# VectorE's exponentials in an attention kernel: seven passes in place of eight, on 16-bit halves

## The chip, the cores and the metric

The kernel runs on one core of a Trainium2 chip. The metric is the device time of one execution in microseconds, less is better. Of the kernel before, three runs gave 2255.68, 2258.31 and 2261.54 us; the median is 2258.31 us.

The engines of the core are named as the profile names them: PE is TensorE (matmuls; PEld its weight loads), ACT is ScalarE, DVE is VectorE, POOL is GpSimd, SP is the engine that issues most DMAs.

## The reference

Four transformer-like blocks follow one another, each a layer norm, an attention and a residual sum. The first and third use a sliding window of 256 positions, the second and fourth full attention without a mask. There are 2048 positions, 640 features, 32 heads of 20 features.

```python
def _A_ref(x, wqkv, wo):
    B, S, D = x.shape
    H = 32; Dh = D // H; W = 256
    ...
    scores = jnp.einsum("bhqd,bhkd->bhqk", q, k) * (Dh ** -0.5)
    idx = jnp.arange(S)
    mask = (idx[:, None] - idx[None, :] >= 0) & (idx[:, None] - idx[None, :] < W)
    scores = jnp.where(mask[None, None], scores, -1e9)
    p = _softmax(scores, axis=-1)
    o = jnp.einsum("bhqk,bhkd->bhqd", p, v)
    return (lambda x, *d: x.transpose(*d))(o, 0, 2, 1, 3).reshape(B, S, D) @ wo
...
x = x + _A_ref(_layernorm(x, axis=-1), A_wqkv, A_wo)
x = x + _B_ref(_layernorm(x, axis=-1), B_wqkv, B_wo)
x = x + _A_ref(_layernorm(x, axis=-1), A_wqkv, A_wo)
x = x + _B_ref(_layernorm(x, axis=-1), B_wqkv, B_wo)
```

`_B_ref` is the same without the mask. All inputs are bf16. What counts here is that every score of the two full blocks goes through an exponential: 2 x 32 x 2048 x 2048 of them.

## The kernel before, in words

**Units.** The work of the attention is cut into units (`Unit`, L672): one block of the network `l`, one chunk `c` of 512 queries, one group `g` of four heads; some units of the second and fourth block are cut further by keys (`PARTS`, L40). For one head and 128 keys a score matmul (L1316) writes a score block, 128 keys by 512 queries in f32, which fills one of the eight PSUM banks. ScalarE takes three score blocks with one instruction, computes the exponential and writes bf16 (L1347). Where bank 6 is free and no other task is ready, it takes four in one instruction, which writes into the tile `ka`. The value matmuls (L1380) multiply the exponentials with the values and sum in bank 7; a column of ones in the values gives the sum of the exponentials. At the end of a unit bank 7 is copied out (L864) and a "tail" divides by that sum (L1053 to L1092).

**Ticks.** The main loop (L1279) makes one tick of each such ScalarE instruction: it issues the score matmuls, the exponential, and then, as far as a credit reaches, pieces of the other work: projections of queries, keys and values (L294 to L298, evacuated by VectorE at L321), output projections (L566), layer norms, tails. Bank 5 (early) and bank 6 serve this other work. All orders are fixed when the program is built: every engine runs its own list in order, and waits for the others by semaphores.

**The blocks that go aside.** ScalarE's exponentials are many, so a fixed set of score blocks of the full attention goes to VectorE: `self.aside` (L676 to L686) lists two blocks a unit in the second network block and four or six in the fourth. Together these are 48 and 106 blocks, handled in 24 and 53 pairs. `t_side` (L897) is the generator that issues VectorE's passes for one pair. A `yield` with a number says what a pass costs in credit (0.7 or 1.2); `side_step` (L956) goes on with the generator only while the credit is positive. The credit grows by 0.4 a tick in the second network block, and by 1.1 (0.95 in the last chunk) in the fourth (L1402). In the second block of the network the score blocks come with a tile of the main loop at fixed ticks (L1320 to L1330); in the fourth they have a score matmul of their own into bank 6 (L912), issued on odd ticks when the bank is free (L1286), and the bank then counts as taken for two ticks. At the end of the unit `side_done` (L998) issues whatever passes of the unit are still missing, and the value matmuls of L1389 take the results.

**The eight passes of a pair, before.** VectorE has no exponential, so e^s is built as 2^t with t = s times log2(e). Two passes (L918, one for each score block of 512 columns) scale the scores by 2^23 log2(e) and write them as 32-bit integers, so that the upper 9 bits are the whole part and the lower 23 the fraction. L923 masks the fraction out and puts an exponent to it, so that it can be read as an f32; L928 masks the whole part out and shifts it to where an exponent is. Four passes with two inputs follow on 1024 columns of f32: L933, L937 and L941 evaluate a polynomial in the fraction, and L949 does the last step of it, multiplies by the power of two and writes bf16. The three work tiles `xi`, `xm`, `xw` are 1024 columns of f32 each; they lie in `raw_o` in the second network block and in `xnT` tiles in the fourth, and the results in `raw_o`, `ka` or `qa`, which is how the profile names them.

Of the kernel before, what the change touches and what calls it, by code (L numbers as in the profile page):

```python
# [9 lines left out]
BF16 = mybir.dt.bfloat16  # L10
F32 = mybir.dt.float32
I32 = mybir.dt.int32
ALU = mybir.AluOpType
ACT = mybir.ActivationFunctionType

# [8 lines left out]
C = 512  # L24
NC = S // C
EPS = 1e-5
SCALE = DH ** -0.5
# [2 lines left out]

E23 = 2.0 ** 23
LOG2E = 1.4426950408889634
EA, EB, EC, ED = -0.10468731, 1.17604568, 0.83196789, 0.24582313
KA = 18
SIDE_RATE = 1.1
QA = 4
# [8 lines left out]
def kernel(  # L47
# [58 lines left out]
    op = ps[:, 7, :]  # L106
# [23 lines left out]
    def load_wop(w, dense):  # L130
# [8 lines left out]
    nc.gpsimd.affine_select(  # L139
        out=ident[:], in_=ident[:], compare_op=ALU.not_equal, fill=1.0,  # L140
        base=0, pattern=[[-1, P]], channel_multiplier=1,
# [5 lines left out]
    for m, b, ge in (  # L147
# [5 lines left out]
        nc.gpsimd.affine_select(  # L153
            out=v, in_=v, compare_op=ALU.is_ge if ge else ALU.is_gt, fill=0.0,
            base=0, pattern=[[1 if ge else -1, P]], channel_multiplier=-1 if ge else 1,
# [4 lines left out]
    def other_constants():  # L160
# [7 lines left out]
        for u in range(2):  # L168
# [4 lines left out]
            nc.vector.tensor_tensor(  # L173
                out=sp16[r], in0=sp32[r, 0, :], in1=sp32[r, 1, :], op=ALU.add
            )
# [215 lines left out]
    def t_ln(l, c):  # L391
# [3 lines left out]
        for n in (1, 0):  # L395
# [6 lines left out]
        nc.gpsimd.tensor_scalar(  # L402
            out=rstd[:], in0=mv[:, :, 1], scalar1=EPS, scalar2=1.0, op0=ALU.add, op1=ALU.mult
        )
        nc.gpsimd.tensor_tensor(out=rstd[:], in0=rstd[:], in1=nhalf[:], op=ALU.pow)
        yield ("wait", 2)
        nmr = lnp.tile([P, 4], F32, name="nmr", tag="nmr")
        nc.vector.scalar_tensor_tensor(
            out=nmr[:], in0=mv[:, :, 0], scalar=-1.0, in1=rstd[:], op0=ALU.mult, op1=ALU.mult
        )  # L410
# [476 lines left out]
    def side_early():  # L887

        b = part_o["t"]
        side["tiles"] = [b[:, 2 * n : 2 * n + 2, :].rearrange("p a b -> p (a b)") for n in range(3)]  # L890
        side["out"] = deque(
            b[:, n, :].bitcast(BF16).rearrange("p (a b) -> p a b", a=2) for n in (6, 7)
        )
        side["gen"] = t_side()
        side_step(False)

    def t_side():  # L897

        V = nc.vector
        while aside:  # L900
            u = aside[0]
            for pair in range(len(u.aside) // 2):
                while id(u) not in loaded or (u.l == 3 and not side["late"]):
                    yield None
                for i in range(2):
                    yield "bank"
                    xi, xm, xw = side["tiles"]
                    if u.l == 3:
                        mseq[0] += 1
                        mfree[6] = (state["tick"] + 2, mseq[0])  # L910
                        kc, j = u.aside[2 * pair + i]
                        nc.tensor.matmul(  # L912
                            ps[:, 6, :], lhsT=u.k(kc, j), rhs=u.q(j, 0, 4), start=True, stop=True
                        )
                        side["psum"] = ps[:, 6, :]
                    scored = side.setdefault("scored", {})
                    scored[id(u)] = scored.get(id(u), 0) + 1
                    V.tensor_scalar(  # L918
                        out=xi.bitcast(I32)[:, i * C : (i + 1) * C], in0=side["psum"],
                        scalar1=SCALE * LOG2E * E23, scalar2=-128.0 * E23, op0=ALU.mult, op1=ALU.max,  # L920
                    )
                    yield 0.7
                V.tensor_scalar(  # L923
                    out=xm.bitcast(I32), in0=xi.bitcast(I32), scalar1=0x7FFFFF, scalar2=0x3E800000,
                    op0=ALU.bitwise_and, op1=ALU.bitwise_or,
                )
                yield 0.7
                V.tensor_scalar(  # L928
                    out=xi.bitcast(I32), in0=xi.bitcast(I32), scalar1=0x7F800000,
                    scalar2=0x40000000, op0=ALU.bitwise_and, op1=ALU.bitwise_xor,  # L930
                )
                yield 0.7
                V.scalar_tensor_tensor(  # L933
                    out=xw, in0=xm, scalar=EA, in1=xm, op0=ALU.add, op1=ALU.mult
                )
                yield 1.2
                V.scalar_tensor_tensor(  # L937
                    out=xm, in0=xw, scalar=EB, in1=xm, op0=ALU.mult, op1=ALU.add
                )
                yield 1.2  # L940
                V.scalar_tensor_tensor(  # L941
                    out=xw, in0=xw, scalar=EC, in1=xm, op0=ALU.add, op1=ALU.mult
                )
                yield 1.2
                while not side["out"]:
                    yield None
                pt = side["out"].popleft()
                po = pt.rearrange("p a b -> p (a b)")
                V.scalar_tensor_tensor(  # L949
                    out=po, in0=xw, scalar=ED, in1=xi, op0=ALU.add, op1=ALU.mult  # L950
                )
                side_out.setdefault(id(u), []).append(pt)
                yield 1.2
            aside.popleft()

    def side_step(bank):  # L956
# [246 lines left out]
    with tc.manual_schedule():  # L1203
# [75 lines left out]
        while ended is None or t < ended + 8:  # L1279
# [3 lines left out]
            if t < len(tiles) or banks:  # L1283
# [58 lines left out]
                while i < n_b:  # L1342
                    b0 = cur[i][3]
                    k = i
                    while k < n_b and cur[k][3] == b0:
                        k += 1
                    nc.scalar.activation(  # L1347
                        out=pt[:, i:k, b0 * P :], in_=sp[:, i:k, b0 * P :],
# [56 lines left out]
            if t > 0 and masked is not None:  # L1405
                cur_, pt_ = masked
                i = 0
                while i < len(cur_):
# [5 lines left out]
                    for b in ((3,), (1, 2), (0,))[m] if split else ():  # L1414
                        if b < b0:
# [4 lines left out]
                            out=v, in_=v, compare_op=ALU.is_gt if later else ALU.is_ge, fill=0.0,  # L1420
# [3 lines left out]
                    if split and m != 1:  # L1424
# [5 lines left out]
                            out=pt_[:, i:k, cols], in0=pt_[:, i:k, cols], in1=mv_, op=ALU.mult  # L1430
                        )
                    elif m is not None and not split:
# [5 lines left out]
                            out=pt_[:, i:k, cols], in0=pt_[:, i:k, cols], in1=mv_, op=ALU.mult  # L1438
# [38 lines left out]
```

## Time and profile before

One execution was profiled. Its span, from the first to the last instruction, is 2253.6 us; the trace records no longer time for it. The table gives the three stretches that matter: the first is that of the second network block's aside passes, the last that of the fourth's.

| | whole span | 493 to 1310 us | 1310 to 1600 us | 1600 to 2240 us |
|---|---|---|---|---|
| length, us | 2253.6 | 817 | 290 | 640 |
| ACT busy, us | 2159.6 | 795.9 | 281.2 | 635.4 |
| PE busy, us | 1946.9 | 704.5 | 246.5 | 543.9 |
| DVE busy, us | 1253.3 | 427.1 | 100.2 | 448.1 |
| POOL busy, us | 484.2 | 170.7 | 71.3 | 0.0 |
| granted PE clock | 0.99 | 1.00 | 1.00 | 0.99 |

The rows of the aside passes, as the profile groups them (both tiles together):

| line | what | count | mean, us |
|---|---|---|---|
| L918 | scale, f32 in PSUM to int32, 512 columns | 154 | 0.69 |
| L923, L928 | mask, int32, 1024 columns | 77 each | 0.69 |
| L933, L937, L941 | two inputs, f32, 1024 columns | 77 each | 1.22 |
| L949 | two inputs, f32 to bf16, 1024 columns | 77 | 1.22 |

How to read it: "busy" is the time in which an engine runs at least one instruction. PE's instructions overlap and their ends are modelled, so 86% busy is not 86% of its peak. A wait is put down to the semaphore that came last. An engine that is idle costs nothing unless the path that ends last goes through it.

### The profile page before, as it was taken

How to read it: one execution, taken by the hardware profiler on the slowest of the kernel's cores; microseconds unless marked ns; L12 is line 12 of the kernel's file. 1: busy time of each engine (PE TensorE's matmuls, PEld its weight loads, DVE VectorE, ACT ScalarE, POOL GpSimd, SP SyncE). 2: the span in 40 equal slices, each digit the busy share in tenths (PEclk: the TensorE clock that was granted, in tenths of full speed). 3: DMA queues.
4: the chain of work that ended last, by engine and by line, in shares of the span. 5: the costliest groups of instructions: out<-in, count | busy, mean ns of one | idle time of the engine just before them, and what ended most of it. 6: DMA issues, size and time to landing. Idle time of an engine off the chain costs nothing.

```text
span 2253.6 us, 71223 instructions
## 1 busy us (share of the span) xinstructions
PE 1946.9 (86%) x30991; PEld 775.9 (34%) x30991; DVE 1253.3 (56%) x2150; ACT 2159.6 (96%) x1736; POOL 484.2 (21%) x950
## 2 busy tenths in 40 slices
PE   8999998988888888888888888898888888888887
PEld 4444443334333333333333443342322222222222
DVE  6656564436454555455553643242577667776666
ACT  7899899999999999999899999999999999999997
POOL 6674544201111124111331123312000000000000
PEclk9999999999999999999999999999999999999999
DMA  6233323422111233012320143113211111111100
GB/s 196 74 102 84 91 78 91 104 70 69 54 34 28 65 91 87 15 34 62 97 78 15 23 115 95 29 26 89 64 52 31 31 40 34 31 31 47 39 19 16
DMA packets 88408, 137.15 MB, mean 61 GB/s; under 512 B 20766, under 2 KB 63486, under 8 KB 88094
## 3 DMA queue, kind: packets, MB, share of 16 engines
q1 hardware_dynamic: 68878, 79.43, 13.2%
q0 software_dynamic: 19216, 53.17, 8.1%
q8 instruction: 242, 3.96, 0.8%
q14 instruction: 72, 0.59, 0.1%
HBM read 99.52 MB, written 27.79 MB: 56 GB/s over the span
## 4 chain that ended last, share of the span: by engine, by line
ACT 46%; PE 25%; issue 16%; DVE 10%; POOL 1%; DMA 1%; SPq 0%; ACTq 0%; DVEq 0%; POOLq 0%
ACT pt L1347 44%; PE ps L298 15%; PE ps L1316 6%; PE ps L1380 2%; ACT ka L1347 1%; DVE on L1092 1%; DVE st L321 1%; DVE x_sb L566 1%; PE ps L1088 1%; PE ps L435 1%; DVE pt L1429 1%; DVE va L321 1%; DVE vs L321 0%; DVE xnT L937 0%; DVE xnT L933 0%
## 5 line engine op out<-in xcount | busy, mean ns | idle before, releaser
L1347 ACT ACTIVATE pt<-ps 128x1536 bf16<-128x1536 f32 (+2 forms) x1634 | 2085.3, 1456 | 62.2 <-PE ps L1316 50.8
L298 PE MATMUL ps<-masks,ident 128*32 128x512 bf16 x6420 | 551.6, 388 | 114.3 <-ACT pt L1347 59.9
L1316 PE MATMUL ps<-qt,kt 32*128 32x512 bf16 x3990 | 545.3, 384 | 92.7 <-ACT pt L1347 84.9
L1380 PE MATMUL ps<-pt,vt 128*21 128x512 bf16 x3838 | 393.2, 382 | 0.1
L1316 PEld LDWEIGHTS <-kt 32*128 32x128 bf16 x3990 | 165.0, 91 | 551.4 <-issue 536.1
L1419 POOL TENSOR_SCALAR_AFFINE_SELECT pt<-pt 128x256 bf16<-128x256 bf16 (+2 forms) x505 | 216.3, 450 | 373.6 <-ACT pt L1347 333.1
L298 PEld LDWEIGHTS <-ident 128*32 128x32 bf16 x6420 | 165.9, 94 | 363.0 <-issue 350.0
L298 PE MATMUL ps<-xnT,wqk 128*32 128x512 bf16 x3320 | 220.6, 383 | 16.3 <-DVE st L321 8.1
L1429 DVE TENSOR_TENSOR pt<-pt,masks 128x512 bf16<-128x512 bf16 (+4 forms) x267 | 114.3, 440 | 177.7 <-ACT pt L1347 175.9
L321 DVE CAST st<-ps 128x512 bf16<-128x512 f32 x134 | 92.7, 692 | 197.9 <-PE ps L298 197.7
L298 PE MATMUL ps<-wop,on 128*32 128x320 bf16 x3712 | 156.9, 301 | 13.9 <-DVE x_sb L566 8.8
L918 DVE TENSOR_SCALAR xnT<-ps 128x512 int32<-128x512 f32 x106 | 73.3, 692 | 163.2 <-PE ps L912 162.3
L1316 PE MATMUL ps<-qa,ka 32*128 32x384 bf16 (+2 forms) x1408 | 118.2, 277 | 32.6 <-ACT pt L1347 29.7
L1380 PEld LDWEIGHTS <-vt 128*21 128x21 bf16 x3942 | 105.7, 91 | 115.3 <-issue 74.4
L298 PEld LDWEIGHTS <-on 128*32 128x32 bf16 x5760 | 116.6, 95 | 76.2 <-issue 54.1
L1092 DVE TENSOR_TENSOR on<-on,ps 128x512 bf16<-128x512 bf16 x128 | 86.4, 684 | 72.9 <-PE ps L1088 71.0
L298 PE MATMUL ps<-wv,xnT 128*32 128x320 bf16 x2560 | 112.4, 301 | 9.7 <-DVE on L1092 2.2
L566 DVE TENSOR_TENSOR x_sb<-x_sb,ps 128x320 bf16<-128x320 bf16 x120 | 58.2, 485 | 107.6 <-PE ps L298 107.5
L298 PEld LDWEIGHTS <-wqk 128*32 128x32 bf16 x3320 | 79.6, 96 | 110.9 <-issue 59.3
L864 DVE CAST on<-ps 128x512 bf16<-128x512 f32 x112 | 77.0, 687 | 44.4 <-PE ps L1380 29.7
L1316 PEld LDWEIGHTS <-ka 32*128 32x128 bf16 x1408 | 43.6, 92 | 116.7 <-issue 108.9
L402 POOL TENSOR_SCALAR rstd<-mv 128x4 f32<-128x4 f32 x15 | 3.7, 249 | 363.8 <-DVE mv L389 355.6
(101 smaller groups left out, 1655.3 us busy)
## 6 DMA issues: line engine op xcount, KB each, us to landing
vt<-v_d SPq DMA_DIRECT2D x48, 336.0 KB
kt<-k_d SPq DMA_DIRECT2D x192, 80.0 KB
wqk<-in_B_wqkv_dram POOLq DMA_DIRECT2D x80, 160.0 KB, 3.5
wqk<-in_A_wqkv_dram POOLq DMA_DIRECT2D x70, 160.0 KB, 3.6
k_d<-st POOLq DMA_DIRECT2D x75, 128.0 KB, 2.5
q_d<-st POOLq DMA_DIRECT2D x75, 128.0 KB, 2.5
qt<-q_d SPq DMA_DIRECT2D x384, 20.0 KB
v_d<-vs POOLq DMA_DIRECT2D x16, 336.0 KB, 3.6
```

Of the source, the lines that this page charges most:

```text
L298: nc.tensor.matmul(out_[r], lhsT=lhsT[:, r], rhs=rhs, start=start, stop=stop)
L321: nc.vector.tensor_copy(out=out_, in_=in_)
L435: nc.tensor.transpose(out=trp[32 * j : 32 * j + 32, dc, :], in_=xn[:, a : a + 32], identity=ident[:],)
L566: nc.vector.tensor_tensor(out=xv, in0=had, in1=yp, op=ALU.add)
L864: nc.vector.tensor_copy(out=oT, in_=op)
L918: V.tensor_scalar(out=xi.bitcast(I32)[:, i * C : (i + 1) * C], in0=side["psum"], scalar1=SCALE * LOG2E * E23, scalar2=-128.0 * E23, op0=AL ...
L1092: nc.vector.tensor_tensor(out=oT, in0=oT, in1=zb, op=ALU.mult)
L1316: nc.tensor.matmul(sp[:, i, col * P : (col + qn) * P], lhsT=u.k(kc, j), rhs=u.q(j, q0, qn), start=True, stop=True,)
L1347: nc.scalar.activation(out=pt[:, i:k, b0 * P :], in_=sp[:, i:k, b0 * P :], func=ACT.Exp, scale=SCALE,)
L1380: nc.tensor.matmul(op[32 * j : 32 * j + VW, q0 * P : (q0 + qn) * P], lhsT=u.v(kc, j), rhs=pg[:, i, col * P : (col + qn) * P], start=(first ...
L1419: nc.gpsimd.affine_select(out=v, in_=v, compare_op=ALU.is_gt if later else ALU.is_ge, fill=0.0, base=0, pattern=[[0, k - i], [-1 if later ...
L1429: nc.vector.tensor_tensor(out=pt_[:, i:k, cols], in0=pt_[:, i:k, cols], in1=mv_, op=ALU.mult)
```

## The change

The passes of a pair are written anew. The two conversions (before L918) keep their shape but scale by 2^16 log2(e), so the integer's upper halfword is the whole part and its lower halfword the fraction. The fraction is read as every other unsigned halfword (`[:, 0::2]`), scaled and shifted into `xm` as f32. The whole part is read as every other signed halfword (`[:, 1::2]`), 127 is added and the sum multiplied by 128, and written as 16-bit integers into `power`, a view of the front half of `xw`; read as bf16 that is the power of two. Two passes with two inputs evaluate a cubic in the shifted fraction, the second of them writes bf16 to the result tile. A last pass multiplies the result tile by `power`, bf16 by bf16, in place. The `yield`s of a pair add up to 5.9 in place of 7.6. Which blocks go aside, the credit per tick and all else stay as they are.

```diff
-E23 = 2.0 ** 23
+FIX = 2.0 ** 16
 LOG2E = 1.4426950408889634
-EA, EB, EC, ED = -0.10468731, 1.17604568, 0.83196789, 0.24582313
+E1, E0, EA, EB = 6.520200689873914e-06 * FIX, 0.7855486869812012, -1.118533968925476, 1.5344765186309814
...
                     V.tensor_scalar(
                         out=xi.bitcast(I32)[:, i * C : (i + 1) * C], in0=side["psum"],
-                        scalar1=SCALE * LOG2E * E23, scalar2=-128.0 * E23, op0=ALU.mult, op1=ALU.max,
+                        scalar1=SCALE * LOG2E * FIX, scalar2=-127.0 * FIX, op0=ALU.mult, op1=ALU.max,
                     )
                     yield 0.7
                 V.tensor_scalar(
-                    out=xm.bitcast(I32), in0=xi.bitcast(I32), scalar1=0x7FFFFF, scalar2=0x3E800000,
-                    op0=ALU.bitwise_and, op1=ALU.bitwise_or,
+                    out=xm, in0=xi.bitcast(U16)[:, 0::2],
+                    scalar1=E1 / FIX, scalar2=E0, op0=ALU.mult, op1=ALU.add,
                 )
                 yield 0.7
+                power = xw.bitcast(I16)[:, 0 : 2 * C]
                 V.tensor_scalar(
-                    out=xi.bitcast(I32), in0=xi.bitcast(I32), scalar1=0x7F800000,
-                    scalar2=0x40000000, op0=ALU.bitwise_and, op1=ALU.bitwise_xor,
+                    out=power, in0=xi.bitcast(I16)[:, 1::2],
+                    scalar1=127.0, scalar2=128.0, op0=ALU.add, op1=ALU.mult,
                 )
                 yield 0.7
                 V.scalar_tensor_tensor(
-                    out=xw, in0=xm, scalar=EA, in1=xm, op0=ALU.add, op1=ALU.mult
-                )
-                yield 1.2
-                V.scalar_tensor_tensor(
-                    out=xm, in0=xw, scalar=EB, in1=xm, op0=ALU.mult, op1=ALU.add
-                )
-                yield 1.2
-                V.scalar_tensor_tensor(
-                    out=xw, in0=xw, scalar=EC, in1=xm, op0=ALU.add, op1=ALU.mult
+                    out=xi, in0=xm, scalar=EA, in1=xm, op0=ALU.add, op1=ALU.mult
                 )
                 yield 1.2
...
                 V.scalar_tensor_tensor(
-                    out=po, in0=xw, scalar=ED, in1=xi, op0=ALU.add, op1=ALU.mult
+                    out=po, in0=xi, scalar=EB, in1=xm, op0=ALU.add, op1=ALU.mult
                 )
+                yield 1.2
+                V.tensor_tensor(out=po, in0=po, in1=power.bitcast(BF16), op=ALU.mult)
                 side_out.setdefault(id(u), []).append(pt)
-                yield 1.2
+                yield 0.7
```

## The prediction

> **What bounds the kernel now.** I read the busy times of the page first, then its stretch-by-stretch table with borders where the changed code starts and stops (493 to 1310 us and 1600 to 2240 us, from the first and last starts of its lines), then the waits of ScalarE and TensorE inside these stretches, and last who waits for the changed code.
>
> ```profile
> PE 1946.9 (86%) x30991; PEld 775.9 (34%) x30991; DVE 1253.3 (56%) x2150; ACT 2159.6 (96%) x1736; POOL 484.2 (21%) x950
> ```
> ```profile
> 493.00:1310.00 817.00, 704.50 (x11372) 291.36 (x11369) 427.12 (x755) 795.94 (x625) 170.66 (x319) 1.00 0.21 56
> 1310.00:1600.00 290.00, 246.53 (x4047) 104.92 (x4039) 100.18 (x207) 281.22 (x208) 71.28 (x128) 1.00 0.25 69
> 1600.00:2240.00 640.00, 543.93 (x7083) 172.50 (x7081) 448.11 (x554) 635.39 (x464) 0.00 (x0) 0.99 0.12 34
> ```
>
> The columns are length, then busy time of PE, PEld, DVE, ACT and POOL. ScalarE (ACT) is busy for 97.4% of the first stretch with VectorE exponentials, and for 99.3% of the second. VectorE (DVE), whose work is changed, is busy for 52% and 70%. ScalarE's exponentials are the floor. Their number is fixed by the lists of score blocks that go aside, and the diff doesn't touch these lists: no block moves from ScalarE to VectorE. So the change can win only ScalarE's idle time after 493 us, as far as VectorE causes it.
>
> ScalarE's waits, first in 493 to 1310 us, then in 1600 to 2240 us:
>
> ```profile
> ACT pt L1347 <- PE ps L1316: 18.1, 43, 0.9
> ACT pt L1347 <- POOL pt L1419: 1.0, 1, 1.0
> ACT pt L1347 <- DVE on L1092: 0.5, 1, 0.5
> ACT pt L1347 <- ACT pt L1347: 0.4, 2, 0.2
> ```
> ```profile
> ACT pt L1347 <- PE ps L1316: 3.6, 9, 0.9
> ```
>
> That is 20.0 and 3.6 us: TensorE's score matmuls come late. TensorE itself waits for VectorE in the first stretch mainly here:
>
> ```profile
> PE ps L298 <- DVE st L321: 13.7, 45, 0.5
> PE ps L298 <- DVE x_sb L566: 5.0, 12, 1.1
> PE ps L298 <- DVE on L1092: 4.0, 11, 0.8
> ```
>
> These are evacuations of a PSUM bank, not the exponentials. The first is 0.3 us a time and at most 0.5, so behind a 1.22 us pass of the exponentials it rarely stands long. The consumer of the exponentials is the value matmul of line 1389. Of the last pass's line the trace says
>
> ```profile
> who waited for it (us, times):
> ```
>
> with nothing below it: nobody ever waited for that result. Nor does the first block of the tail: the last L949 ends at 2241.8 us, and the last ScalarE exponential, which the next matmuls need anyway, ends at 2242.5 us.
>
> **The change, part by part.** All durations are from this one profiled execution.
>
> *Before, per pair of blocks* (77 pairs: 24 in the first stretch, 53 in the second, one with its last passes at the very end): two L918 at 0.692 us, L923 and L928 at 0.694 us each, and four passes (L933, L937, L941, L949) at 1.22 us: 1.384 + 1.388 + 4.88 = 7.65 us. Times 77 that is 589 us, and the groups of these lines add up to the same.
>
> *Conversion of the scores (2 per pair).* Only its constants change: same shape, same row, 0.692 us.
>
> *Two masking passes out, two strided halfword passes in.* The trace has no pass that reads every other halfword. Its nearest row from below is L923 (1024 elements, one input, all in SBUF): 0.69 us; from above the 1024-element passes with two inputs: 1.22 us. I take 0.69, because these too have one tensor input in SBUF and a constant pair, as L923 and L928 have. The Trainium skill, "Vector Engine (DVE) Microarchitecture Reference", section 5.1, says that the two-port mode asks for one SBUF source, an SBUF destination and an even outermost dimension, and names no step or type; by it such a pass would stay at 0.69 us. The same page's section 5.2 speaks against the change: it measured 1.73 ns an element for a source that leaves its adjacent words at every element; by that, as an estimate, 1.77 us a pass and a pair of some 8.1 us, more than now. Here every 4-byte word is touched in turn, which is not that case, and no run here shows it yet.
>
> *Four two-input f32 passes become two.* Minus 2.44 us. Their shapes are those of L933 and L949, so 1.22 us each stays.
>
> *One 16-bit product in.* The nearest rows are the mask multiplications of line 1429, bf16 times bf16: 256 elements 337 ns, 768 elements 588 ns, so 0.49 ns an element, and 1024 elements give 588 + 256 × 0.49 = 713 ns. Bounds: 0.59 us (the 768-element row as it is) and 1.22 us (the f32 pass of that length). I take 0.71.
>
> *Sum per pair*: 1.384 + 2 × 0.694 + 2 × 1.22 + 0.71 = 5.92 us, so 1.73 us less; at the upper bounds 1.384 + 4 × 1.22 + 1.22 = 7.48 us, 0.17 us less; with the product at its lower bound 5.80 us, 1.85 us less. VectorE loses 77 × 1.73 = 133 us (13 to 142), and stands near 1120 us busy. **None of that lies on the path that sets the end**: it runs beside ScalarE, whose exponentials hide it. Were that cover gone, all of it would count.
>
> *What the path gets.* I went through ScalarE's gaps after 493 us one by one in the trace (those over 50 ns). In the first stretch 11.2 us of them have, in the 3.5 us ahead, a TensorE wait for VectorE; in 7.5 us of these one of the seven lines also ran for over 0.3 us in the 3 us ahead. In the second stretch both sums are 2.6 us. So 10.1 us at most is what the exponentials' passes could have caused. A pass removed takes away its share of such collisions: 1.73 of 7.65, 23%, of 10.1 us, that is 2.3 us. Nothing at all is possible: between the two stretches, from 1310 to 1600 us, where no such pass runs, ScalarE's wait for TensorE is 8.4 us in 290, or 2.9 us in 100, against 18.1 in 817, or 2.2 in 100, with them. Where such a stall goes, the next late thing is again ScalarE's previous exponential.
>
> *The pacing (the yields).* A pair costs 7.6 credits before and 2 × 0.7 + 0.7 + 0.7 + 1.2 + 1.2 + 0.7 = 5.9 after. In the first stretch credit comes at 0.4 a tick, so passes are issued over 15 ticks in place of 19; the two score blocks still come from fixed tiles. In the second it is 1.1 a tick: 5.4 ticks in place of 6.9 for a pair, until the units loaded have no blocks left; then VectorE rests. The count of single score matmuls (L912, 106) is unchanged. They come closer together, and take PSUM bank 6 for two ticks each, so the projections and tails that share that bank are issued some ticks earlier or later; over a unit of 19 or 20 ticks it is the same number of ticks. Which odd ticks get a four-block exponential changes with it (25 in the second stretch now), but this is worth little: start to start a four-block one takes about 1.76 us and back-to-back three-block ones take 1.331 us, so 0.440 us and 0.444 us a block, and ten more or fewer give under 0.2 us.
>
> *New wait, queues.* The value matmul now waits for the product and no longer for the pass ahead of it. Behind the matmul on TensorE stand the tail of the unit and the next scores; but the chain ends earlier, and nobody waited for it before. No DMA moves by the code itself, none is added, and GpSimd has no part in the changed passes.
>
> **Sum.** The profiled execution's span is 2253.6 us; the trace holds no longer time for it. The median of the three runs, 2258.3 us, lies 4.7 us above, which I take as what lies around the span. 2253.6 - 2.3 + 4.7 = 2256.0 us, or 0.1% below the median shown.
>
> **Rivals.**
> *Faster than that.* A lighter VectorE frees TensorE's banks sooner also where the last 3 us show no such pass, through a queue that was late earlier. For it: 11.2 + 2.6 = 13.8 us of gaps follow a TensorE wait for VectorE. Against it: the stretch without the passes has no fewer gaps. If all go: 2258.3 - 13.8 = 2244.5 us.
> *Slower: issue outruns VectorE.* The pacing now believes in 5.9 us a pair. In the second stretch that is 5.36 ticks of some 1.36 us (73.5 exponentials in 100 us), 7.3 us; VectorE's other work there is 448 - 404 = 44 us of 640, 6.9%, so it can give 6.8 us to a pair. That is the point that decides: if a pair takes over 6.8 us, VectorE falls behind what is issued, and bank evacuations queued behind it hold TensorE's scores. At the upper bounds, 7.48 us, it needs 7.48 / 0.931 = 8.0 us, 0.7 us too late at each of 53 pairs, 37 us; TensorE's 15% of spare time and the rests at the units' ends should take two thirds (my choice), which leaves 12 us: 2270 us. For it: no row shows a strided pass. Against it: on average a pair has 640 / 53 = 12 us, so arrears can't pile up over more than two or three pairs.
> *It doesn't do what it says.* The passes grow so long that a pair stays at 7.5 us, but the slack takes it: nothing moves, 2258 us.
>
> **How the numbers follow.** A difference under about 0.3% (6.8 us) is about what a measurement of this kernel can't tell from no change. The forecast of 2256.0 gets 71%; its own range goes from 2248 (all 10.1 us won) to 2261.5 (nothing won, and the slowest run shown). The rival without effect gets 4%, the faster one 16%, the slower one 9%. Within 0.3%: 0.75; faster 0.16; slower 0.09. Two in ten outside cuts most of the slower rival and the far end of the faster one: 2246 to 2263 us.
>
> **What would show it.** VectorE's busy time falls to about 1120 us and ScalarE's stays within 2 us of 2159.6. The two strided passes read 0.69 us each, the product 0.71. ScalarE's waits for L1316 fall from 18.1 us by two or so in the stretch to 1310 us. Nobody waits for the product's line. I am wrong if a strided pass takes over 1.13 us with the product as I have it (5.92 + 2 × 0.44 = 6.8), if ScalarE's idle time in the second stretch grows, or if TensorE's waits at L298 and L912 for VectorE grow; wrong to the good side if the stretch to 1310 us loses over 10 us of ScalarE's idle time.

## The result, and the profile after

The changed kernel takes 2267.34 us in the median of 12 runs (2263.37 to 2275.53), the kernel before, run beside it, 2256.36 us in 12 runs. The ratio is 1.0051, 95% interval 1.0038 to 1.0064: **slower** by 11 us, half a per cent and clear of the noise, where 2 us less was forecast. The time lies outside the range of 2246 to 2263 us. The profiled execution has a span of 2264.5 us against 2253.6.

The first row of the page after, and its stretches (length, then busy time of PE, PEld, DVE, ACT, POOL, granted clock, DMA share, GB/s):

```profile
PE 1955.3 (86%) x30991; PEld 776.1 (34%) x30991; DVE 1118.4 (49%) x2073; ACT 2158.3 (95%) x1737; POOL 484.1 (21%) x950
```
```profile
493.00:1310.00 817.00, 706.72 (x11399) 291.63 (x11391) 384.57 (x731) 797.67 (x627) 172.00 (x319) 1.00 0.21 56
1310.00:1600.00 290.00, 246.72 (x4052) 104.88 (x4044) 101.81 (x210) 281.59 (x208) 70.55 (x127) 1.00 0.25 68
1600.00:2240.00 640.00, 541.61 (x6945) 170.34 (x6941) 355.40 (x500) 621.67 (x456) 0.00 (x0) 0.98 0.11 33
```

VectorE (DVE) has 134.9 us less to do and ScalarE (ACT) as much as before, yet the stretch of the fourth network block has lost 13.7 us of ScalarE's busy time: ScalarE stood still there. The passes are as cheap as hoped; of their lines the trace of after says

```profile
L925 DVE TENSOR_SCALAR xnT<-xnT x53: 685/694/696, 1599.0 to 2191.2; 128x1024 f32<-128x1024 uint16 x53
L931 DVE TENSOR_SCALAR xnT<-xnT x53: 684/686/690, 1599.6 to 2191.9; 128x1024 int16<-128x1024 int16 x53
L948 DVE TENSOR_TENSOR ka<-ka,xnT x33: 677/691/693, 1603.5 to 2202.7; 128x1024 bf16<-128x1024 bf16 x33
```

(shortest, median, longest in ns). So what made ScalarE stand still? Its waits in 1600 to 2250 us, and under them TensorE's in 1600 to 2240 us:

```profile
ACT pt L1344 <- PE ps L1313: 17.8, 13, 4.3
```
```profile
PE ps L300 <- ACT pt L1344: 48.8, 111, 0.9
PE ps L1313 <- ACT pt L1344: 12.0, 39, 0.6
PE ps L914 <- DMA kt<-k_d: 11.7, 6, 3.9
PE ps L300 <- DMA on<-on: 3.6, 1, 3.6
```

17.8 us where 3.6 were. The third row is new: L914 is the single score matmul of a side block (L912 before), and it waits for a **load of keys**. Before, in the same stretch, that matmul waited for VectorE alone, 4.0 us in all:

```profile
PE ps L912 <- DVE on L1092: 2.5, 5, 1.0
PE ps L912 <- DVE rT L1071: 1.0, 2, 0.5
PE ps L912 <- DVE x_sb L566: 0.5, 1, 0.5
```

The fourth row is one more new wait for a DMA, of an output projection for a copy within `on`, 3.6 us once. The two make 15.3 us, and from the first single score matmul to ScalarE's last exponential the stretch is 657.5 us long in place of 644.1.

One of the six in the timeline, first TensorE (PE), then the engine that issues loads (SP). Columns: start, length, engine, line, what, count, in brackets the idle time before it:

```profile
2000.62 0.39 PE L1313 MATMUL ps<-qt,kt 32*128 32x512 bf16 x3 [0.37 <-ACT pt L1344]
2004.95 0.60 PE L914 MATMUL ps<-qt,kt 32*128 32x512 bf16 x1 [3.94 <-DMA kt<-k_d]
2005.48 0.61 PE L1377 MATMUL ps<-pt,vt 128*21 128x512 bf16 x4
2005.88 1.07 PE L300 MATMUL ps<-masks,ident 128*32 128x512 bf16 x8
2006.88 0.61 PE L1313 MATMUL ps<-qt,kt 32*128 32x512 bf16 x3
```
```profile
2000.79 0.43 SPq L780 DMA_DIRECT2D vt<-v_d  x1
2001.27 0.35 SPq L792 DMA_DIRECT2D qt<-q_d  x1
2001.66 0.33 SPq L794 DMA_DIRECT2D kt<-k_d  x1
```

The keys that L914 needs are issued from 2001.66 us on, after L914 has reached the head of TensorE's list at 2001.01. Everything behind it, the value matmuls and the next scores for ScalarE, waits 3.9 us with it. In the other five the load had been issued 0.3 to 2.5 us before TensorE came to it; in all six L914 starts 2.9 to 3.3 us after the unit's first load of keys was issued. Then comes a second loss: the matmuls run at half speed. The granted clock (third column from the right) in stretches around it:

```profile
1990.00:2000.00 10.00, 9.17 (x114) 2.65 (x106) 6.19 (x10) 10.00 (x8) 0.00 (x0) 1.00 0.06 14
2000.00:2005.00 5.00, 0.69 (x8) 0.24 (x4) 2.16 (x3) 3.25 (x3) 0.00 (x0) 0.79 0.47 138
2005.00:2009.00 4.00, 4.00 (x31) 0.85 (x32) 0.69 (x1) 1.40 (x1) 0.00 (x0) 0.50 0.09 26
```

At 0.50 the three score matmuls take 0.61 us in place of 0.39 and the eight of L300 1.07 in place of some 0.6.

**Theory A.** The cheaper yields let the generator run ahead until it scores blocks of a unit whose load is issued but not landed. The program counts a unit as loaded as soon as the load stands in SP's list, whenever SP comes to it. The lead in ticks (1.36 us each) from a unit's load to its first side block can be counted in the order in which each program is built: before, 23 to 39 ticks for all units but the first, which has 6; after, 6 to 18, and 1 or 2 from the second unit of the last chunk on. All six waits for keys fall to these last units. The passes themselves are innocent. **Theory B** (the rival): the passes hold something up, whatever the pace. **A rival to A's place**: the single score matmuls crowd bank 6, whether the load has landed or not.

### The profile page after: what moved, and what is told of

Read it like the earlier page. It is cut to its first block, busy times and chain, and to the rows that moved or that the text cites. A ratio compares the mean times of both kernels' runs of the same rounds, so it can differ in the third digit from the quotient of the medians.

```text
span 2264.5 us, 71155 instructions
## 1 busy us (share of the span) xinstructions
PE 1955.3 (86%) x30991; PEld 776.1 (34%) x30991; DVE 1118.4 (49%) x2073; ACT 2158.3 (95%) x1737; POOL 484.1 (21%) x950
## 3 DMA queue, kind: packets, MB, share of 16 engines
q1 hardware_dynamic: 68878, 79.43, 12.7%
## 4 chain that ended last, share of the span: by engine, by line
ACT 48%; PE 24%; issue 16%; DVE 7%; DMA 2%; POOL 1%; SPq 0%; ACTq 0%; DVEq 0%; POOLq 0%
ACT pt L1344 47%; PE ps L300 15%; PE ps L1313 6%; PE ps L1377 2%; ACT ka L1344 1%; DVE st L323 1%; DVE on L1089 1%; DMA kt<-k_d 1%; DVE x_sb L568 1%; DVE pt L1426 1%; DVE va L323 1%; PE ps L1085 0%; DVE vs L323 0%; DMA wqk<-in_A_wqkv_dram 0%; POOL pt L1416 0%
## 5 line engine op out<-in xcount | busy, mean ns | idle before, releaser
L300 PE MATMUL ps<-masks,ident 128*32 128x512 bf16 x6420 | 551.7, 388 | 100.9 <-ACT pt L1344 57.4
L300 PEld LDWEIGHTS <-ident 128*32 128x32 bf16 x6420 | 163.6, 94 | 343.8 <-issue 332.1
L300 PE MATMUL ps<-xnT,wqk 128*32 128x512 bf16 x3320 | 221.3, 384 | 16.5 <-DVE st L323 8.1
L300 PE MATMUL ps<-wop,on 128*32 128x320 bf16 x3712 | 157.9, 302 | 13.3 <-DVE x_sb L568 5.1
L300 PEld LDWEIGHTS <-on 128*32 128x32 bf16 x5760 | 116.5, 95 | 76.8 <-issue 54.6
L300 PE MATMUL ps<-wv,xnT 128*32 128x320 bf16 x2560 | 112.5, 301 | 8.9 <-DVE on L1089 2.2
L300 PEld LDWEIGHTS <-wqk 128*32 128x32 bf16 x3320 | 79.6, 96 | 111.5 <-issue 58.8
```

Of the source, the lines that this page charges most:

```text
L300: nc.tensor.matmul(out_[r], lhsT=lhsT[:, r], rhs=rhs, start=start, stop=stop)
```

## The experiments

The edits are shown in short form.

**e1: the new passes at the old pace.**

```diff
-yield 0.7 / 0.7 / 1.2 / 1.2 / 0.7     (the changed kernel's chain)
+yield 1.0 / 1.0 / 1.6 / 1.6 / 1.0
```

> The changed kernel with the old pace: the five yields of the chain are 1.0, 1.0, 1.6, 1.6, 1.0, so a pair costs 7.6 credits again; the seven passes stay. Theory A (the cheaper yields let VectorE's generator run ahead to units whose loads are issued and not landed, and its score matmul then blocks TensorE's queue): TensorE's waits of the single score matmul for the load of kt, 11.7 us after the change, are gone, ScalarE's wait for scores from 1600 to 2240 us is back from 17.8 to about 4 us, and the time is that of the kernel before or 2 us less, ratio 0.998 to 1.001. Theory B (the new passes themselves hold something up): it stays at 1.004 to 1.006.

Measured 0.9952 (0.9936 to 0.9968), 2247.7 us. The leads in ticks are exactly those of the kernel before, and TensorE waits for no load. ScalarE's waits of e1 in 1600 to 2240 us, and under them the longest of TensorE's there but for two rows in which L300 waits for ScalarE:

```profile
ACT pt L1344 <- PE ps L1313: 1.1, 4, 0.4
```
```profile
PE ps L1313 <- ACT pt L1344: 8.3, 31, 0.4
PE ps L300 <- DVE on L1089: 1.9, 5, 0.6
PE ps L300 <- DVE x_sb L568: 1.9, 4, 0.9
PE ps L914 <- DVE on L1089: 0.8, 2, 0.4
```

The passes alone make the kernel faster, by more than A said (0.998 at best); B falls.

**e2: the old passes at the new pace.**

```diff
-yield 0.7 / 0.7 / 1.2 / 1.2 / 1.2 / 1.2     (the chain of the kernel before)
+yield 0.5 / 0.5 / 0.8 / 0.9 / 0.9 / 0.9
```

> The kernel before with the new pace alone: its six passes after the conversions cost 0.5, 0.5, 0.8, 0.9, 0.9, 0.9 credits, 5.9 a pair with the conversions; the passes themselves are the old ones. Theory A: the waits for kt come as in the changed kernel (about 10 us, some 6 of them), ratio 1.004 to 1.008, the upper half because VectorE also falls behind what is issued (7.65 us a pair where the pace gives 7.3). Theory B: without the new passes it stays within 0.2% of the kernel before.

Measured 1.0301 (1.0285 to 1.0317), 2326.5 us. TensorE's waits of e2 in 1600 to 2240 us:

```profile
PE ps L298 <- DVE rT L1071: 13.0, 11, 1.7
PE ps L912 <- DMA kt<-k_d: 12.7, 7, 4.2
PE ps L298 <- DVE on L1092: 11.4, 9, 1.6
PE ps L298 <- DVE rz L1053: 10.9, 10, 1.3
```

The load's wait is back without any new pass, at about its size after the change (12.7 us against 11.7): the pace alone makes it. ScalarE waits 58.7 us for scores in this stretch. The other three rows are waits for VectorE, 35.3 us: it is behind what is issued. That these small evacuations of the tails stand behind 1.22 us passes is my reading; I did not follow them one by one. A said 1.008 at most; the direction holds, the size of the second part was far too low.

**e3 and e5: the new passes and the new pace, with a gate.** A unit's blocks may be scored only some ticks after its load was issued.

```diff
-while id(u) not in loaded or (u.l == 3 and not side["late"]):
+while (
+    id(u) not in loaded or (u.l == 3 and not side["late"])
+    or (u.l == 3 and state["tick"] < loaded_at[id(u)] + 14)      (22 in e5)
+):
...
 loaded.add(id(u))
+loaded_at[id(u)] = state["tick"]
```

> The changed kernel with its new pace, but in the fourth network block the generator may take a unit only 14 ticks (about 19 us) after its load was issued. Theory A: the waits for kt are gone, ScalarE's wait for scores from 1600 to 2240 us is about 4 us, ratio 0.998 to 1.001, as with the old pace. A rival to A (the closer spacing of the single score matmuls on bank 6 is what costs, by fewer four-block exponentials or late tails): the spacing within a unit is that of the changed kernel, so 1.003 to 1.005. Theory B: 1.004 to 1.006.

> The changed kernel with its new pace and a gate of 22 ticks (about 30 us) after the load in place of 14. With 14 ticks the single runs spread from 2247 to 2262 us, with the old pace, whose leads are 23 to 39 ticks, only from 2243 to 2251. Theory A with the lead as what counts: the ratio comes to that of the old pace, 0.994 to 0.997, and the runs lie within some 8 us. Rival (the lead of 14 is enough, and the old pace won for its even spacing of passes): 0.997 to 0.9995 as with 14 ticks.

Measured 0.9983 (0.9968 to 0.9998) with 14 ticks and 0.9973 (0.9963 to 0.9983) with 22. In neither does TensorE wait for kt (L919, the single score matmul of these two, waits for a load of queries for 1.0 us in all with 14 ticks). ScalarE's waits in 1600 to 2240 us with 14 ticks:

```profile
ACT pt L1349 <- PE ps L1318: 2.0, 4, 0.8
```

Within a unit the blocks follow one another as fast as in the changed kernel, so the crowding of bank 6 isn't what cost, and the last rival falls (it asked for 1.003 or more). The lead decides whether TensorE waits for the keys. But 22 ticks don't reach the old pace's 0.9952. e5's 0.9973 lies among the values of its rival, by which the old pace won for its even spacing, and its runs spread from 2247 to 2259 us, nearly as wide as those of 14 ticks (2247 to 2262).

**e9, e10 and e1 once more: what the old pace has over the gates.** e9 restores the old pace by the credit of the fourth block's stretch alone, e10 adds the old pace of the early stretch to the gate of 22, e1b is e1 again as their yardstick on the same chip as these two.

```diff
-SIDE_RATE = 1.1        and 0.95 in the last chunk
+SIDE_RATE = 0.854      and 0.7375                       (e9)
-0.4 a tick in the early stretch
+0.3105                                                  (e10, on top of e5)
```

> The changed kernel as it is, cheap yields too, but with less credit a tick in the fourth network block alone: 0.854 in place of 1.1 and 0.7375 in place of 0.95, the old ones times 5.9/7.6. The early stretch keeps the new pace, the late one has the old leads of 23 to 39 ticks but for the last units (11 to 30). Theory A, with the late leads as all that counts: ratio 0.994 to 0.997 as with the old pace throughout, and no wait for kt. Rival (the early stretch's new pace costs some of it): 0.997 to 0.999 as with the gates.

> The gate of 22 ticks with the old pace in the early stretch alone (0.3105 credit a tick in place of 0.4, that is 0.4 x 5.9/7.6). If the early stretch's pace is what the gates lack against the old pace: 0.994 to 0.9965. If not: 0.9965 to 0.998, as with the gate of 22 alone.

> The changed kernel at the old pace once more, beside the two others on the same chip, as their yardstick: 0.994 to 0.997 by its first measurement; if it lies at 0.997 or more, the old pace and the gates don't differ and the first measurement was at the edge of its spread.

Measured e9 0.9971 (0.9958 to 0.9985), e10 0.9975 (0.9966 to 0.9985), e1b 0.9958 (0.9946 to 0.9971). e9 decides nothing: its value lies 0.0001 above what A said, at the lower end of the rival's range, its interval reaches into both, and it overlaps e1b's. e10 speaks against the early pace. The old pace (e1, e1b) is 0.0013 to 0.0031, some 3 to 7 us, ahead of e3, e5, e9 and e10, in both of its measurements. Even spacing doesn't explain it either: by the order in which the program is built, e9 has the old spacing of the score matmuls in all but the last chunk. In the profiles ScalarE waits 1.1 and 0.5 us from 1600 to 2250 us at the old pace and 2.2 to 4.0 us in the other four, so part of the difference lies there. The intervals touch or overlap, and what makes the difference is **open**.

**e4 and e6: the gate, and more blocks for VectorE's free time.** The change frees 135 us of VectorE; each block that goes aside takes 0.444 us off ScalarE.

```diff
-if l == 3 and (c < 3 and g % 2 and (c, g) != (2, 7)):     (six blocks aside, else four)
+if l == 3 and (c < 3 and (c, g) != (2, 7)):               (e4: 14 blocks more, gate 14)
+if l == 3 and (c, g) < (3, 6):                            (e6: 28 blocks more, gate 20)
```

In e6 the credit of 1.1 a tick also lasts up to the last chunk's sixth unit.

> The kernel of the gate of 14 ticks, with seven more pairs of blocks going to VectorE: six blocks aside in every unit of the second and third chunk of the fourth network block but the last, in place of every other. Theory A: 14 blocks of 0.444 us leave ScalarE, so 6.2 us less than with the gate alone, ratio 0.995 to 0.998; VectorE's busy time from 1600 to 2240 us grows by 7 x 5.9 = 41 us. Theory B: above 1.0.

> New pace, gate of 20 ticks, and six blocks aside in every unit of the last three chunks of the fourth network block but its last two units (the credit of 1.1 a tick up to there): 28 blocks more than the changed kernel. Theory A: against the gate alone 28 x 0.444 = 12.4 us leave ScalarE, so 2236 to 2240 us, ratio 0.990 to 0.993; VectorE's busy time grows by 14 x 5.9 = 83 us to some 1200 us. If VectorE's arrears or bank 6 take it back, 0.994 to 0.998 and TensorE's waits for VectorE in 1600 to 2240 us over 10 us.

Measured e4 0.9944 (0.993 to 0.9959), somewhat better than its 0.995 to 0.998, and e6 0.9929 (0.9917 to 0.9941), 2241.8 us: the fastest kernel here, 1.2% below the changed one by the two ratios. The stretch of e6 shows where it comes from, with VectorE at 439.7 us. ScalarE has less to do and is as dense as before, with waits of 3.1 us against 3.6:

```profile
1600.00:2240.00 640.00, 552.98 (x7089) 172.54 (x7085) 439.69 (x615) 623.98 (x462) 0.00 (x0) 0.99 0.12 35
```

**e7: more blocks at the old pace.** e1 with e4's line.

> The changed passes at the old pace (7.6 credits a pair), with the 7 pairs more aside of the second and third chunk. Such a unit asks 22.8 credits, 19 ticks give 21, so passes are left to the end of the unit and issued at once. Theory A: no wait for kt; 6.2 us of exponentials leave ScalarE, 0.992 to 0.993 if VectorE's real 5.9 us a pair absorbs the rush, 0.995 or more if TensorE then waits for the results at the units' ends (value matmuls of the side blocks).

Measured 1.0102 (1.0087 to 1.0116). The open branch of the expectation came, with its sign, TensorE's waits for the results at the units' ends; that the kernel would be slower than before wasn't expected. TensorE's longest waits for VectorE of e7 in 1600 to 2240 us (L1386 are the value matmuls of the side blocks):

```profile
PE ps L914 <- DVE xnT L920: 11.9, 10, 4.4
PE ps L1386 <- DVE ka L948: 9.5, 7, 2.4
PE ps L1386 <- DVE qa L948: 5.5, 3, 3.3
```

VectorE had the time, 60% busy; the credit kept it from being used. With the same blocks, the new pace and a gate, e4 has 0.9944. Too dear a yield makes the results late, too cheap a one makes the requests early.

**e8: more blocks in the second network block too.** e6, with `if l == 1 and False:` turned to `if l == 1:` and 0.55 credits a tick there.

> As the kernel with six blocks aside in all chunks and the gate of 20, and in the second network block four blocks aside a unit in place of two (24 pairs more, credit 0.55 a tick in place of 0.4 there). 48 x 0.444 = 21 us of exponentials leave ScalarE there, but each such tick carries only two blocks beside the side block, and VectorE is busy for 47% + 142/817 = 64% of that stretch, with evacuations and mask products behind its passes. If the stretch stays bound by ScalarE: 0.981 to 0.985. If TensorE's or VectorE's other work becomes its bound: 0.988 to 0.995, with ScalarE's waits in 493 to 1310 us up from 18 us to over 30.

Measured 1.0166 (1.0145 to 1.0187), worse than the worse case. ScalarE's wait for scores in 493 to 1310 us is 74.4 us, where the changed kernel has 16.3, and TensorE waits longer for VectorE there, for evacuations and side conversions:

```profile
PE ps L300 <- DVE on L1094: 16.8, 23, 2.1
PE ps L1318 <- DVE raw_o L925: 8.6, 9, 1.7
```

In the changed kernel the first of these is 3.8 us, and the second isn't there. VectorE is 59% busy. It isn't full; by these waits it is late for single instructions that others need at once. That this makes the whole loss is not shown: the granted clock of the stretch also falls, from 1.00 to 0.94.

## Why the prediction was wrong

**What bounds the kernel** held: ScalarE's exponentials do, and the change could only touch ScalarE's idle time.

**Durations** held. A strided pass has 0.69 us, the product 0.69 where I took 0.71, so the pair is 1.38 + 1.38 + 2.44 + 0.69 = 5.89 us where I had 5.92, and VectorE's 1118.4 us stand beside "near 1120". A pass over every other halfword runs like the dense L923. The Trainium skill, "Vector Engine (DVE) Microarchitecture Reference", section 5.1, agrees with that: its conditions for the two-port mode name no step. The dear estimate by its section 5.2 (1.77 us) did not come.

**What the path gets**: right in sign, too small in size. The term was 2.3 us; e1 and e1b, which have the passes without the pace, give 0.9952 and 0.9958, 9.5 to 11 us. My share rule took 23% of the 10.1 us of stalls behind a side pass. In the profiles of e1 and e1b ScalarE's waits in the two stretches fall by 5.6 and 6.6 us (20.0 to 16.9 and 16.5, 3.6 to 1.1 and 0.5), more than half of them, so a share in proportion was too little. (In between, where no such pass runs, the 8.4 us are 11.6 in e1 and 8.7 in e1b.) In the changed kernel itself the first stretch gains 2.0 us. Where the rest of the 9.5 us comes from is open.

**The pacing** is the step that failed. I wrote "5.4 ticks in place of 6.9 for a pair, until the units loaded have no blocks left; then VectorE rests", and priced only bank 6 and the width of ScalarE's instructions. I saw that units run out, but took "loaded" as the program's word for it: it means that the DMA is issued. With slack on VectorE the generator moves up to that edge, in the last chunk to 1 or 2 ticks from it, and the next thing late is the load. In my sum this step stood at nothing. It cost 11.7 us of TensorE's waits for keys in the profiled run, half speed around the longest of them, and it took the ratio from e1's 0.9952 to 1.0051. The 3.6 us for `on` go with the new pace too (e2 has 6.0 us of them, e1 and e1b none), by a path that I did not trace. "No DMA moves by the code itself" was true and beside the point: the reader moved towards it. I listed what waits behind the value matmul, and never asked what the single score matmul itself waits for.

**Four-block exponentials** fell from 26 to 21 in the whole kernel, which at 0.004 us a block is nothing, as said.

**The rivals.** The slower one, issue outrunning VectorE, gave 2270 us, near the time measured, but by the wrong mechanism: a pair takes 5.89 us, under its point of 6.8, and TensorE's waits for VectorE at L300 did not grow (11.7 us from 1600 to 2240 us before, at L298, and 1.7 after). e2 shows that the mechanism exists: with a pair of 7.65 us at the new pace, over that point, the kernel loses 3.0%, some 68 us, of which the load's waits are the smaller part; my price of 12 us for it was much too low, and that a pair has 12 us on average was no protection. Of the signs I named, "ScalarE's idle time in the second stretch grows" is the one that came.

## What to carry to other kernels

When a producer that is paced by a cost table becomes cheaper, ask what it runs into at full speed: here it ran ahead to a load that was issued and not landed, and one waiting matmul blocked an in-order queue that fed the bound engine. A flag that says "loaded" when a DMA is issued is safe only as long as something slow stands between it and the first use. Change the work and its pace apart, in two runs, before the change is judged: here the new passes alone are worth -0.5%, and the new pace adds 1% to them and 3% to the old passes.

## What the runs showed of the hardware that I had not expected

A stall of TensorE can cost more than its length. After 3.9 us without a matmul the granted clock was 0.50 for about 4 us (shown above). Around waits of 2.7 us at 2143 and 2175 us it fell to 0.50 and 0.52 as well, in the second case 1.4 us after the matmuls had begun again:

```profile
2143.00:2146.00 3.00, 2.60 (x20) 0.63 (x24) 0.69 (x1) 0.38 (x1) 0.00 (x0) 0.50 0.27 92
2178.00:2180.50 2.50, 2.50 (x19) 0.39 (x15) 1.74 (x3) 1.68 (x2) 0.00 (x0) 0.52 0.00 0
```

That the waits made it fall is likely, not shown. It also falls without such a wait: in the profile before it was 0.50 here, though no wait of TensorE in the 7 us ahead was longer than 0.7 us:

```profile
1771.50:1778.00 6.50, 6.50 (x49) 1.12 (x45) 3.38 (x5) 4.79 (x5) 0.00 (x0) 0.50 0.05 13
```

The Trainium skill, "TensorE: Matmul & The Clock Gate", Part 1, names an idle window of about 3.4 us for the drop to half rate; the drops here came at shorter waits than that too.
